# A chunked attention with a gated feed-forward: decay rows stored at a step of 6656 bytes, and a new order of the opening

## The chip, the cores and the metric

The kernel runs on one core of one Trainium2 chip. TensorE (PE in the views) multiplies, VectorE (DVE), ScalarE (ACT) and GpSimd (POOL) work on elements, SyncE (SP) issues transfers, and 16 DMA engines carry them from the device's memory. The metric is the device time of one execution in microseconds (us).

## The reference

An attention with decays runs over 4 batches, 8 heads and 768 tokens with 48 channels each. Its output, laid out as 3072 tokens of 384 channels, goes through a gated feed-forward of 1536 hidden channels, whose three weight matrices arrive as float64.

```python
for t in range(S):
    cur = np.einsum('bhd,bhe->bhde', u[None] * kt, vt)
    y[:, :, t] = np.einsum('bhd,bhde->bhe', rt, state + cur)
    state = wt[:, :, :, None] * state + np.einsum('bhd,bhe->bhde', kt, vt)
...
gate = 1.0 / (1.0 + np.exp(-(x @ w_gate)))
val = x @ w_val
return (gate * val @ w_out).astype(np.float32)
```

## The kernel before

The tokens are cut into 24 chunks of 128 (6 of each batch; chunk q belongs to batch q mod 4). A chunk needs two transfers: `pin` (decays, k and r, channel by channel, 112 rows of 1544 floats, 675.5 KB, L281) and `tok` (r, k and v token by token, 576 KB, L286). On VectorE it costs a scan, a reciprocal and a product (L321, L325, L327), a second scan and product (L338, L343), a reduction `a` for the bonus (L310), two masks `at` (L402), the state (L432), two `bon` (L448) and the rest of x (L466). On TensorE it costs `pk`, the sums `pv`, the scores `pa` (L370, L380), the value product and the transposed x.

The feed-forward goes by words: word f is 128 of the 1536 hidden channels with all three matrices, 1152 KB of float64. VectorE rebuilds float32 from the bits in `full` (L251, L255, L259). ScalarE checks the word's range (the guard, L245 and L246) and casts it to its high part (L264), VectorE subtracts that for the low part (`w`, L267), and then the word is ready. Every product is three matmuls of high and low parts: `pg` and `pu` (L474) against x, the sigmoid `sg` of `pg` on ScalarE (L485), its product with `pu` on VectorE (L492, named sg too), the high part `hh` on ScalarE (L496), the low part `hl` on VectorE (L500), and `po` on TensorE (L509).

Chunks 0 to 12 and the feed-forward of the first 8 chunks' rows form the opening, some 245 us. There the feed-forward works on two chunks at a time (`GROUPS`, four half groups), beside the words' arrival. After it a hand-written loop takes four chunks' rows at once with the next chunks' attention woven in.

The opening's order comes from a planner, class `Plan`. Each step is given to it with its engine, a cost in us, the steps that it needs, the buffers that it takes and gives back (`ROOM`) and a rank. The planner plays time forward: an engine that is free takes the step of lowest rank whose needs are met and whose buffers are free, and writes its instructions. So the costs and ranks set each engine's fixed order, and nothing else in the program. `TURNS` gives the ranks of chunks (c) and words (w), `LAGS` those of the four half groups, and `COMES` the order in which SP issues the transfers (p is pin, t is tok, w a word). SP issues them in just that order: one that waits for a buffer (two of pin, two of tok; a word has its own) holds up all behind it. On the chip each engine executes its list in order and waits by semaphore for the others.

In the lists of steps below a name carries the chunk's or the word's number and, behind a low line, a number of the program: full2_441 belongs to word 2, eg3_518 to chunk 3, a02_425 is `a` of chunk 2 (its tile is called a0), x0 holds the rows of chunks 0 to 3. sg0_0_3 and hl0_0_3 are the first half group (chunks 0 and 1) and word 3. Decays, k and r lie in the array `dec`, which the host writes ahead of the launch; the function `kernel` packs it.

Of the kernel before, what the change touches and what calls it, by code (L numbers as in the profile page):

```python
# [34 lines left out]
COMES = "p0 t0 ub w0 p1 p2 t1 w1 w2 p3 t2 t3 w3 w4 w5 t4 p4 w6 w7 w8 w9 w10 w11 p5 t5 t6 p6 t7 p7 p8 t8 t9 p9 p10 p11 t10 t11 p12 p13 t12 t13"
GROUPS = [(0, 0, 2), (0, 2, 4), (1, 0, 2), (1, 2, 4)]
LAGS = [0, 6.5, 15, 16]
ROOM = dict(pin=2, tok=2, bon=2, eg=1, ready=2, mid=2, kT=1, at=1, bank=2, x=2, full=1, pg=1, pu=1, unit=4, po0=1, po1=1, po2=1, po3=1)
HC = C // 2
HALVES = [slice(0, HC), slice(HC, C)]  # L40
# [4 lines left out]
def general(ctx: ExitStack, tc: tile.TileContext, dec, tok, wts, u, out, whi, wlo, ident):  # L45
# [44 lines left out]
    values = tok.rearrange("(b c) t (n p o e) -> c n o t b p e", b=B, n=3, o=2, e=D)  # L90
    for c in range(NC_):
        for b in range(B):
            nc.sync.dma_start(d[:, b], dec[b * NC_ + c])
        with tc.For_i(0, C) as i:
            def at(first, step):
                return d[:, :, first:first + NP * step].rearrange("a b (p c) -> a b p c", c=step)[:, :, :, bass.ds(i, 1)].broadcast_to(shape)
            for o in range(2):
                for b in range(B):
                    nc.sync.dma_start(vb[64 * o:64 * o + D, b], values[c, 2, o, bass.ds(i, 1), b].partition_broadcast(D))
            nc.vector.tensor_tensor(out=kv, in0=vb, in1=at(WW, C), op=ALU.mult)  # L100
            nc.vector.tensor_tensor(out=mix, in0=kv, in1=ub, op=ALU.mult)
# [90 lines left out]
def tile_kernel(ctx: ExitStack, tc: tile.TileContext, dec: bass.AP, tok: bass.AP, wts: bass.AP, u: bass.AP, out: bass.AP):  # L192
# [79 lines left out]
    def place(q):  # L272
        return q % B * NC_ + q // B

    def load_pin(q):
        t = p2.tile([L, WW + 2 * NP * C], F32, tag="pin", name=f"pin{q}")
        if q == 0:
            nc.sync.dma_start(t[:, :WW], dec[place(q)][:, :WW])
            nc.sync.dma_start(t[:, WW:], dec[place(q)][:, WW:])
        else:  # L280
            nc.sync.dma_start(t, dec[place(q)])  # L281
        pin[q] = t

    def load_tok(q):
# [253 lines left out]
    add("ub", "SP", 0.6, [], comes["ub"], lambda: nc.sync.dma_start(ub, u.partition_broadcast(P)))  # L538
    for q in range(3 * B + 2):
        k = rank.get(f"c{q}", 99)  # L540
        add(f"pin{q}", "SP", 2.4, [], comes[f"p{q}"], load_pin, q, take=["pin"])
        add(f"tok{q}", "SP", 2.1, [], comes[f"t{q}"], load_tok, q, take=["tok"])
        if q > 3 * B:
            continue
        add(f"b1_{q}", "POOL", 1.0, [f"tok{q}", "ub"], k, bonus1, q, take=["bon"])
        add(f"b2_{q}", "POOL", 1.0, [f"b1_{q}"], k, bonus2, q)
        add(f"b3_{q}", "DVE", 0.55, [f"b2_{q}"], k + 0.3, bonus3, q)
        add(f"b4_{q}", "POOL", 0.83, [f"b3_{q}"], k, bonus4, q)
        add(f"pk{q}", "DVE", 2.07, [f"pin{q}"], k, prep_k, q, take=["eg"])
        old = q >= B  # L550
        if old:
            add(f"fade{q}", "DVE", 0.36, [f"pk{q}", f"keep{q - B}"], k + 0.05, fade, q, take=["ready"])
        add(f"pr{q}", "DVE", 1.93, [f"pk{q}"], k + 0.1, prep_r, q)
        add(f"guard{q}", "ACT", 1.26, [f"pr{q}", old and f"fade{q}"], k + 0.5, guard, q, give=["eg"])
        if q == 3 * B:
            continue
        add(f"tk{q}", "PE", 0.4, [f"pk{q}"], k + 0.1, turn_k, q, take=["bank", "kT"])
        add(f"kT{q}", "ACT", 0.52, [f"tk{q}"], k + 0.1, take_k, q, give=["bank"])
        add(f"sm{q}", "PE", 0.55, [f"kT{q}", f"tok{q}"], k + 0.15, sums, q, take=["bank", "bank"], give=["kT"])
        add(f"mid{q}", "DVE" if old else "ACT", 0.36, [f"sm{q}", old and f"fade{q}"], k + 0.12, middle, q, take=["mid"], give=["bank"])  # L560
        add(f"keep{q}", "DVE", 0.36, [f"mid{q}"], k + 0.15, keep, q, give=["bank"])
        add(f"sc{q}", "PE", 1.1, [f"pr{q}", f"mid{q}"], k + 0.2, scores, q, take=["bank", "bank", "at"], give=["pin"] + ["ready"] * old)
        add(f"m0{q}", "DVE", 0.42, [f"sc{q}"], k + 0.2, mask, q, 0)
        add(f"m1{q}", "DVE", 0.42, [f"m0{q}"], k + 0.2, mask, q, 1)
        add(f"mx{q}", "PE", 0.5, [f"m1{q}"], k + 0.3, mix, q, give=["at"])
        add(f"mid{q}done", None, 0, [f"sc{q}", f"keep{q}"], k, give=["mid"])
        add(f"y0{q}", "DVE", 0.36, [f"mx{q}", f"b4_{q}"], k + 0.3, take_y, q, 0, give=["bank"])
        add(f"y1{q}", "DVE", 0.36, [f"y0{q}"], k + 0.3, take_y, q, 1, give=["bank"])
        first = q % B == 0
        add(f"tx{q}", "PE", 0.33, [f"y1{q}", q % B and f"tx{q - 1}"], k + 0.4, turn_x, q, take=["bank"] + ["x"] * first, give=["bon"])  # L570
        add(f"xh{q}", "ACT", 0.68, [f"tx{q}"], k, take_x, q)
        add(f"xl{q}", "DVE", 0.56, [f"xh{q}"], k, rest_x, q, give=["bank"])
        add(f"tok{q}done", None, 0, [f"mx{q}", f"sm{q}", f"b4_{q}", q % B and f"tok{q - 1}done"], k, give=["tok"])
    for f in range(NFF):
        k = rank[f"w{f}"]
        add(f"words{f}", "SP", 4.2, [], comes[f"w{f}"], fetch, f)
        add(f"wg{f}", "ACT", 2.8, [f"words{f}", f and f"wg{f - 1}"], k, w_guard, f)
        add(f"wb{f}", "DVE", 0.76, [f"words{f}", f and f"wb{f - 1}"], k, w_body, f, take=["full"])
        add(f"ws{f}", "DVE", 1.36, [f"wb{f}"], k, w_sign, f)
        add(f"wt{f}", "DVE", 1.36, [f"ws{f}"], k, w_tail, f)  # L580
        add(f"wh{f}", "ACT", 1.15, [f"wt{f}", f"wg{f}"], k, w_hi, f)
        add(f"wl{f}", "DVE", 1.3, [f"wh{f}"], k, w_lo, f, give=["full"])
# [101 lines left out]
```

## Time and profile before

| | |
|---|---|
| median of 3 runs | 605.04 us (603.53 to 608.01) |
| the profiled execution | 603.9 us, of which the span is 602.2 |
| TensorE busy | 558.7 us, 93% of the span |
| VectorE busy | 332.6 us, 55% |
| ScalarE busy | 201.6 us, 33% |
| GpSimd busy | 96.7 us, 16% |
| moved by DMA | 50.85 MB |

The profile is one execution, taken by the hardware profiler. Busy time is a sum over stages of different character, so a share of the whole span says little about one stage; the windows of the trace give the same by stretches. A wait in the timeline of an engine stands in brackets behind the instruction that waited, with what ended it. An instruction's duration can overlap the next one's start by some hundredths of a us.

### The profile page before, as it was taken

To read this page: it belongs to the slowest core of one execution; us is meant where nothing else is said; L and a number is where in the kernel's file an instruction comes from. 1 tells how busy PE (TensorE), PEld (TensorE's weight loads), DVE (VectorE), ACT (ScalarE), POOL (GpSimd) and SP (SyncE) were. 2 spreads that over 40 slices of the span, in tenths; PEclk is the share of its full clock that TensorE was granted. 3 is DMA by queue.
4 is the path that set the end of the run, shared out by engine and by line. 5 is a ranking of instruction groups with operands and counts; after the bars stand their busy time and mean duration, and the time that the engine had idled before them with its cause. 6 is when DMAs were issued, how large, how long until landed. Compare 5 with 4: busy or idle time off the path is not lost. (4 is left out here: it accounts for less than half of the span.)

```text
span 602.2 us, 14593 instructions
## 1 busy us (share of the span) xinstructions
PE 558.7 (93%) x6474; PEld 498.4 (83%) x6474; DVE 332.6 (55%) x570; ACT 201.6 (33%) x402; POOL 96.7 (16%) x86
## 2 busy tenths in 40 slices
PE   4475899999999999899999999999999999999994
PEld 3365799999999999788888888888888888888883
DVE  4989879989685653254554554554454453221220
ACT  3648683444333322312222322222321221222212
POOL 3352111102120502002201211211211210000000
PEclk9999699999999999999999999999999999999997
DMA  8788920033233130122033033022033000100001
GB/s 250 250 327 290 347 95 1 1 87 83 72 121 126 50 125 3 53 86 86 3 87 87 28 112 86 2 86 87 35 106 87 1 1 2 54 1 0 1 1 57
DMA packets 12055, 50.85 MB, mean 84 GB/s; under 512 B 1376, under 2 KB 4576, under 8 KB 10448
## 3 DMA queue, kind: packets, MB, share of 16 engines
q1 hardware_dynamic: 8528, 45.11, 23.4%
q10 hardware_dynamic: 3456, 4.72, 2.2%
q8 instruction: 53, 0.87, 0.6%
q14 instruction: 18, 0.15, 0.1%
HBM read 45.11 MB, written 4.72 MB: 83 GB/s over the span
## 5 line engine op out<-in xcount | busy, mean ns | idle before, releaser
L474 PE MATMUL pg<-x,w 128*128 128x256 f32 (+1 forms) x864 | 171.6, 344 | 2.1 <-DVE w L267 2.1
L474 PE MATMUL pu<-x,w 128*128 128x256 f32 (+1 forms) x864 | 170.5, 342 | 0.0
L474 PEld LDWEIGHTS pg<-x,w 128*128 128x128 f32 x864 | 138.3, 193 | 17.8 <-DVE w L267 2.2
L474 PEld LDWEIGHTS pu<-x,w 128*128 128x128 f32 x864 | 136.2, 191 | 17.3
L509 PE MATMUL po<-w,hh 128*128 128x384 f32 x576 | 147.7, 337 | 0.0
L492 DVE TENSOR_TENSOR sg<-pu,sg 128x256 f32<-128x256 f32 (+1 forms) x96 | 53.4, 557 | 149.9 <-PE pu L474 148.9
L509 PE MATMUL po<-w,hl 128*128 128x384 f32 x288 | 101.2, 351 | 7.1 <-DVE hl L500 7.0
L496 ACT CAST hh<-sg 128x256 fp32r<-128x256 f32 (+1 forms) x96 | 49.2, 512 | 170.0 <-DVE sg L492 169.6
L509 PEld LDWEIGHTS po<-w,hh 128*128 128x128 f32 x576 | 105.0, 189 | 0.9
L485 ACT ACTIVATE sg<-pg 128x256 f32<-128x256 f32 (+1 forms) x96 | 46.9, 488 | 141.7 <-PE pg L474 140.1
L314 POOL TENSOR_TENSOR bon<-tok,a 128x384 f32<-128x384 f32 x24 | 35.0, 1457 | 282.7 <-DVE a L310 282.7
L500 DVE TENSOR_TENSOR hl<-sg,hh 128x256 fp32r<-128x256 f32 (+1 forms) x96 | 55.7, 580 | 39.0 <-ACT hh L496 39.0
L509 PEld LDWEIGHTS po<-w,hl 128*128 128x128 f32 x288 | 54.3, 189 | 10.4 <-DVE hl L500 8.4
L303 POOL TENSOR_TENSOR bon<-tok,ub 128x384 f32<-128x384 f32 x24 | 32.6, 1358 | 113.4 <-DMA tok<-tok 61.1
L448 DVE TENSOR_TENSOR bon<-pa,bon 128x192 f32<-128x192 f32 x48 | 15.6, 353 | 49.3 <-PE pa L441 49.2
L348 ACT ACTIVATE junk<-eg 112x1032 bf16<-112x1032 f32 x24 | 25.6, 1066 | 30.7 <-DVE eg L338 30.6
L321 DVE TENSOR_TENSOR_SCAN eg<-pin,ends 112x516 f32<-112x516 f32 x24 | 30.0, 1251 | 4.9 <-DMA pin<-dec 4.9
L338 DVE TENSOR_TENSOR_SCAN eg<-pin,heads 112x516 f32<-112x516 f32 x24 | 30.5, 1270 | 0.0
L353 PE MATMUL pk<-ident,pin 112*128 112x112 f32 x96 | 14.7, 278 | 14.1 <-DVE pin L327 10.2
L306 POOL TENSOR_TENSOR bon<-bon,tok 128x384 f32<-128x384 f32 x24 | 27.3, 1136 | 1.7
L441 PE MATMUL pa<-tok,at 64*32 64x48 f32 x1536 | 23.8, 213 | 2.3 <-DVE at L402 2.3
L353 PEld LDWEIGHTS pk<-ident,pin 112*128 112x128 f32 x96 | 11.5, 150 | 17.1 <-issue 9.0
(62 smaller groups left out, 433.8 us busy)
## 6 DMA issues: line engine op xcount, KB each, us to landing
pin<-dec SPq DMA_DIRECT2D x23, 675.5 KB, 5.8
tok<-tok SPq DMA_DIRECT2D x24, 576.0 KB, 5.8
wraw<-wts SPq DMA_DIRECT2D x12, 1152.0 KB, 12.3
y<-o ACTq DMA_DIRECT2D x24, 192.0 KB, 1.9
pin<-dec SPq DMA_DIRECT2D x1, 448.0 KB, 4.3
pin<-dec SPq DMA_DIRECT2D x1, 227.5 KB, 2.9
ub<-u SPq DMA_DIRECT2D x1, 192.0 KB, 6.7
```

What stands on the lines that cost most here:

```text
L303: nc.gpsimd.tensor_tensor(out=bon[q], in0=tk[q][:, 0:DM], in1=ub, op=ALU.mult)
L306: nc.gpsimd.tensor_tensor(out=bon[q], in0=bon[q], in1=tk[q][:, DM:2 * DM], op=ALU.mult)
L314: nc.gpsimd.tensor_tensor(out=by_head(bon[q]), in0=by_head(tk[q][:, 2 * DM:]), in1=a0, op=ALU.mult)
L321: nc.vector.tensor_tensor_scan(out=e[:, 516:0:-1], data0=t[:, 516:0:-1], data1=ends[:, 516:0:-1], initial=0.0, op0=ALU.mult, op1=ALU.add,)
L338: nc.vector.tensor_tensor_scan(out=e[:, WW:WW + 516], data0=t[:, 0:516], data1=heads[:, 0:516], initial=0.0, op0=ALU.mult, op1=ALU.add,)
L353: nc.tensor.transpose(out=t[:, p * L:(p + 1) * L], in_=kk(q)[:, p], identity=ident[:L, :L])
L474: nc.tensor.matmul(t, lhsT=w[f][:, cols], rhs=x[n][:, a, k, i0 * C:i1 * C], start=k == 0 and j == 0, stop=k == NKT - 1 and j == 2)
L485: nc.scalar.activation(sg, hid["g", n, f, i0], AF.Sigmoid)
L492: nc.vector.tensor_tensor(out=sg, in0=hid["u", n, f, i0], in1=sg, op=ALU.mult)
L496: nc.scalar.copy(hh, hid["s", n, f, i0])
L500: nc.vector.tensor_tensor(out=hl, in0=hid["s", n, f, i0], in1=hid["hi", n, f, i0].bitcast(F32), op=ALU.subtract)
L509: nc.tensor.matmul(po[n, i][:, :DM], lhsT=h[:, c], rhs=w[f][:, 2 * DM:], start=f == 0 and j == 0, stop=f == NFF - 1 and j == 2,)
```

## The change

The rows of `dec` are padded from 1544 floats to `WR` = 1664, so that they begin 6656 bytes apart and not 6176 (13 x 512 bytes); the loads cut the pad off again. The order is made anew with other ranks (`TURNS`, `COMES`, `LAGS`) and other costs of three kinds of transfer in the planner (pin 2.4 to 2.6, tok 2.1 to 1.8, word 4.2 to 3.0). Each engine executes the same instructions as before, in another order. The line numbers of the changed kernel are one higher (L267 becomes L268).

```diff
@@ -27,14 +27,15 @@
 L = 112
 W1 = C + 1
 WW = 520
+WR = 1664
 NFF = DFF // P
 NKT = DM // P
 TINY = 2.0 ** -14
 LEAST = float.fromhex("0x1.2p-15")
-TURNS = "c0 w0 c1 w1 c2 w2 w3 w4 w5 c3 w6 w7 w8 c4 w9 w10 w11 c5 c6 c7 c8 c9 c10 c11 c12"
-COMES = "p0 t0 ub w0 p1 p2 t1 w1 w2 p3 t2 t3 w3 w4 w5 t4 p4 w6 w7 w8 w9 w10 w11 p5 t5 t6 p6 t7 p7 p8 t8 t9 p9 p10 p11 t10 t11 p12 p13 t12 t13"
+TURNS = "c0 w0 w1 c1 w2 c2 w3 w4 c3 w5 w6 w7 w8 c4 w9 w10 w11 c5 c6 c7 c8 c9 c10 c11 c12"
+COMES = "p0 ub t0 w0 p1 t1 p2 w1 w2 p3 t2 t3 w3 w4 w5 t4 w6 p4 w7 w8 w9 w10 t5 p5 t6 p6 p7 w11 t7 p8 t8 t9 p9 p10 t10 t11 p11 p12 t12 t13 p13"
 GROUPS = [(0, 0, 2), (0, 2, 4), (1, 0, 2), (1, 2, 4)]
-LAGS = [0, 6.5, 15, 16]
+LAGS = [0, 9.0, 15.5, 14.5]
 ROOM = dict(pin=2, tok=2, bon=2, eg=1, ready=2, mid=2, kT=1, at=1, bank=2, x=2, full=1, pg=1, pu=1, unit=4, po0=1, po1=1, po2=1, po3=1)
 HC = C // 2
 HALVES = [slice(0, HC), slice(HC, C)]
@@ -90,7 +91,7 @@
     values = tok.rearrange("(b c) t (n p o e) -> c n o t b p e", b=B, n=3, o=2, e=D)
     for c in range(NC_):
         for b in range(B):
-            nc.sync.dma_start(d[:, b], dec[b * NC_ + c])
+            nc.sync.dma_start(d[:, b], dec[b * NC_ + c][:, :WW + 2 * NP * C])
         with tc.For_i(0, C) as i:
             def at(first, step):
                 return d[:, :, first:first + NP * step].rearrange("a b (p c) -> a b p c", c=step)[:, :, :, bass.ds(i, 1)].broadcast_to(shape)
@@ -276,9 +277,9 @@
         t = p2.tile([L, WW + 2 * NP * C], F32, tag="pin", name=f"pin{q}")
         if q == 0:
             nc.sync.dma_start(t[:, :WW], dec[place(q)][:, :WW])
-            nc.sync.dma_start(t[:, WW:], dec[place(q)][:, WW:])
+            nc.sync.dma_start(t[:, WW:], dec[place(q)][:, WW:WW + 2 * NP * C])
         else:
-            nc.sync.dma_start(t, dec[place(q)])
+            nc.sync.dma_start(t, dec[place(q)][:, :WW + 2 * NP * C])
         pin[q] = t
 
     def load_tok(q):
@@ -538,8 +539,8 @@
     add("ub", "SP", 0.6, [], comes["ub"], lambda: nc.sync.dma_start(ub, u.partition_broadcast(P)))
     for q in range(3 * B + 2):
         k = rank.get(f"c{q}", 99)
-        add(f"pin{q}", "SP", 2.4, [], comes[f"p{q}"], load_pin, q, take=["pin"])
-        add(f"tok{q}", "SP", 2.1, [], comes[f"t{q}"], load_tok, q, take=["tok"])
+        add(f"pin{q}", "SP", 2.6, [], comes[f"p{q}"], load_pin, q, take=["pin"])
+        add(f"tok{q}", "SP", 1.8, [], comes[f"t{q}"], load_tok, q, take=["tok"])
         if q > 3 * B:
             continue
         add(f"b1_{q}", "POOL", 1.0, [f"tok{q}", "ub"], k, bonus1, q, take=["bon"])
@@ -573,7 +574,7 @@
         add(f"tok{q}done", None, 0, [f"mx{q}", f"sm{q}", f"b4_{q}", q % B and f"tok{q - 1}done"], k, give=["tok"])
     for f in range(NFF):
         k = rank[f"w{f}"]
-        add(f"words{f}", "SP", 4.2, [], comes[f"w{f}"], fetch, f)
+        add(f"words{f}", "SP", 3.0, [], comes[f"w{f}"], fetch, f)
         add(f"wg{f}", "ACT", 2.8, [f"words{f}", f and f"wg{f - 1}"], k, w_guard, f)
         add(f"wb{f}", "DVE", 0.76, [f"words{f}", f and f"wb{f - 1}"], k, w_body, f, take=["full"])
         add(f"ws{f}", "DVE", 1.36, [f"wb{f}"], k, w_sign, f)
@@ -664,10 +665,10 @@
         o[:, 64:64 + D] = a[:, 1]
         return o
 
-    dec = np.zeros((NG, L, WW + 2 * NP * C), np.float32)
+    dec = np.zeros((NG, L, WR), np.float32)
     dec[:, :, :NP * W1].reshape(NG, L, NP, W1)[..., 1:] = lanes(inputs["w"], 1.0)
     dec[:, :, WW:WW + NP * C] = lanes(inputs["k"], 0.0).reshape(NG, L, -1)
-    dec[:, :, WW + NP * C:] = lanes(inputs["r"], 0.0).reshape(NG, L, -1)
+    dec[:, :, WW + NP * C:WW + 2 * NP * C] = lanes(inputs["r"], 0.0).reshape(NG, L, -1)
     rows = [inputs[n].transpose(0, 2, 1, 3).reshape(NG, C, H * D) for n in ("r", "k", "v")]
     tok = np.ascontiguousarray(np.concatenate(rows, axis=2))
     ups = [inputs[n].reshape(NKT, P, NFF, P).transpose(2, 1, 0, 3).reshape(NFF, P, DM) for n in ("moe_w_gate", "moe_w_val")]
```

SP's order is the string `COMES`, word for word. Of VectorE's list three places follow, before and then now.

First, the start, from chunk 0's bonus `a` (the seventh step): `at0` are chunk 0's masks, `full0` is word 0.

```order
L310 TENSOR_REDUCE a00_177<-bon0_124 128x8
L402 TENSOR_TENSOR at0_150<-pa0_0_151,after_85 128x256
L402 TENSOR_TENSOR at0_150<-pa0_1_152,after_85 128x256
L251 TENSOR_SCALAR full0_187<-wraw0_113 128x1152
L448 TENSOR_TENSOR bon0_124<-pa0_0_151,bon0_124 128x4x48
L255 SCALAR_TENSOR_TENSOR full0_187<-wraw0_113,full0_187 128x1152
```

```order
L311 TENSOR_REDUCE a00_152<-bon0_122 128x8
L252 TENSOR_SCALAR full0_182<-wraw0_113 128x1152
L403 TENSOR_TENSOR at0_154<-pa0_0_155,after_85 128x256
L256 SCALAR_TENSOR_TENSOR full0_182<-wraw0_113,full0_182 128x1152
L403 TENSOR_TENSOR at0_154<-pa0_1_156,after_85 128x256
L260 SCALAR_TENSOR_TENSOR full0_182<-wraw0_113,full0_182 128x1152
```

Word 0's first two steps stand between and ahead of the masks now; they stood behind them.

Second, around the first hidden rows, from chunk 1's x (step 36 before, 39 now) to sg0_0_0.

```order
L466 TENSOR_TENSOR x0_233<-px1_377,x0_233 128x3x128
L267 TENSOR_TENSOR w1_373<-full1_312,w1_373 128x1152
L310 TENSOR_REDUCE a02_425<-bon2_382 128x8
L432 TENSOR_TENSOR state2_101<-pv2_1_393,mid2_421 112x192
L251 TENSOR_SCALAR full2_441<-wraw2_277 128x1152
L492 TENSOR_TENSOR sg0_0_0_427<-pu0_0_0_429,sg0_0_0_427 128x256
L255 SCALAR_TENSOR_TENSOR full2_441<-wraw2_277,full2_441 128x1152
L500 TENSOR_TENSOR hl0_0_0_487<-sg0_0_0_427,hh0_0_0_475 128x256
```

```order
L467 TENSOR_TENSOR x0_252<-px1_390,x0_252 128x3x128
L260 SCALAR_TENSOR_TENSOR full2_378<-wraw2_254,full2_378 128x1152
L433 TENSOR_TENSOR state2_101<-pv2_1_403,mid2_430 112x192
L311 TENSOR_REDUCE a02_435<-bon2_376 128x8
L322 SCALAR_TENSOR_TENSOR eg3_447<-pin3_322,ends_80 112x516
L326 RECIPROCAL heads_83<-eg3_447 112x4
L328 TENSOR_TENSOR pin3_322<-pin3_322,eg3_447 112x512
L493 TENSOR_TENSOR sg0_0_0_454<-pu0_0_0_437,sg0_0_0_454 128x256
```

Behind that x stand word 1's L260, the state, `a` and the three first steps of chunk 3 now; before it was word 1's last step, `a`, the state and the first step of word 2.

Third, around word 4's last step, w4, up to sg0_0_4; the step ahead of the first row of each list is word 4's L259 (L260).

```order
L448 TENSOR_TENSOR bon3_423<-pa3_0_669,bon3_423 128x4x48
L333 TENSOR_TENSOR ready4_768<-state0_99,eg4_664 112x192
L448 TENSOR_TENSOR bon3_423<-pa3_1_670,bon3_423 128x4x48
L338 SCALAR_TENSOR_TENSOR eg4_664<-pin4_612,heads_83 112x516
L343 TENSOR_TENSOR pin4_612<-pin4_612,eg4_664 112x512
L500 TENSOR_TENSOR hl0_0_3_789<-sg0_0_3_728,hh0_0_3_784 128x256
L267 TENSOR_TENSOR w4_786<-full4_712,w4_786 128x1152
L466 TENSOR_TENSOR x0_233<-px3_780,x0_233 128x3x128
L251 TENSOR_SCALAR full5_814<-wraw5_516 128x1152
L310 TENSOR_REDUCE a04_826<-bon4_619 128x8
L255 SCALAR_TENSOR_TENSOR full5_814<-wraw5_516,full5_814 128x1152
L492 TENSOR_TENSOR sg0_0_4_828<-pu0_0_4_816,sg0_0_4_828 128x256
```

```order
L403 TENSOR_TENSOR at3_689<-pa3_0_690,after_85 128x256
L501 TENSOR_TENSOR hl0_0_3_743<-sg0_0_3_718,hh0_0_3_738 128x256
L403 TENSOR_TENSOR at3_689<-pa3_1_691,after_85 128x256
L334 TENSOR_TENSOR ready4_754<-state0_99,eg4_685 112x192
L268 TENSOR_TENSOR w4_741<-full4_683,w4_741 128x1152
L449 TENSOR_TENSOR bon3_395<-pa3_0_690,bon3_395 128x4x48
L252 TENSOR_SCALAR full5_803<-wraw5_452 128x1152
L449 TENSOR_TENSOR bon3_395<-pa3_1_691,bon3_395 128x4x48
L256 SCALAR_TENSOR_TENSOR full5_803<-wraw5_452,full5_803 128x1152
L339 SCALAR_TENSOR_TENSOR eg4_685<-pin4_624,heads_83 112x516
L344 TENSOR_TENSOR pin4_624<-pin4_624,eg4_685 112x512
L493 TENSOR_TENSOR sg0_0_4_813<-pu0_0_4_822,sg0_0_4_813 128x256
```

Word 4's last step is step 78 and not 81; chunk 4's second scan and product stand behind it, and chunk 3's two `bon` too.

## Rows read from the trace of the kernel before

**Rows 1.** The page of the kernel before: its span, and of each engine the busy time, share of the span and instructions.

```profile
span 602.2 us, 14593 instructions
...
PE 558.7 (93%) x6474; PEld 498.4 (83%) x6474; DVE 332.6 (55%) x570; ACT 201.6 (33%) x402; POOL 96.7 (16%) x86
```

**Rows 2.** Windows of the same trace, 13 to 75 us and 75 to 150 us: length; of each engine the busy time and (instructions); granted TensorE clock, DMA share, GB/s.

```profile
13.00:75.00 62.00, 39.71 (x636) 35.16 (x629) 55.27 (x77) 41.51 (x73) 17.44 (x12) 0.92 0.86 302
...
75.00:150.00 75.00, 74.29 (x973) 71.59 (x972) 67.55 (x107) 36.52 (x75) 10.47 (x9) 1.00 0.18 54
```

**Rows 3.** What VectorE (DVE) waited for between 13 and 75 us: the waiting tile and line, the one waited for, and us in total, times, longest.

```profile
DVE sg L492 <- PE pu L474: 4.2, 3, 1.8
DVE bon L448 <- PE pa L441: 0.9, 2, 0.5
DVE at L402 <- PE pa L380: 0.9, 1, 0.9
DVE x L466 <- ACT x L462: 0.4, 1, 0.4
DVE full L251 <- DMA wraw<-wts: 0.4, 1, 0.4
```

**Rows 4.** Transfers, view of stretches. First line: 57.9 to 66.9 us, in which words alone are moved (queue, packets, MB, share of the 16 engines' time). Second: 204.5 to 210 us, in which one pin alone is moved. Third: 13 to 18 us, a mix of pins, tokens and words. The last two: what was issued between 46.2 and 48.3 us (bytes of each, us from issue to landing): word 6 and pin 4.

```profile
q1 hardware_dynamic: 462, 3.77, 100.3%
...
q1 hardware_dynamic: 128, 0.69, 44.2%
...
q1 hardware_dynamic: 240, 1.17, 98.9%
...
wraw<-wts SPq DMA_DIRECT2D x1, 1152.0 KB, 9.9
pin<-dec SPq DMA_DIRECT2D x1, 675.5 KB, 8.1
```

**Rows 5.** Timeline of VectorE: start in us, duration in us, engine, line, operation, out<-in, shape, and in brackets the idle time before it with what ended it.

```profile
11.87 0.76 DVE L402 TENSOR_TENSOR at<-pa,after 128x256 f32<-128x256 f32 x2 [0.22 <-PE pa L380]
13.01 0.76 DVE L251 TENSOR_SCALAR full<-wraw 128x1152 int32<-128x1152 int32 x1 [0.39 <-DMA wraw<-wts]
...
37.94 0.54 DVE L310 TENSOR_REDUCE a<-bon 128x8 f32<-128x384 f32 x1
38.41 0.34 DVE L432 TENSOR_TENSOR state<-pv,mid 112x192 f32<-112x192 f32 x1
...
40.93 0.43 DVE L492 TENSOR_TENSOR sg<-pu,sg 128x256 f32<-128x256 f32 x1 [1.42 <-PE pu L474]
41.27 1.35 DVE L255 SCALAR_TENSOR_TENSOR full<-wraw,full 128x1152 int32<-128x1152 int32 x1
...
42.87 0.42 DVE L402 TENSOR_TENSOR at<-pa,after 128x256 f32<-128x256 f32 x1
...
46.39 0.18 DVE L325 RECIPROCAL heads<-eg 112x4 f32<-112x4 f32 x1
46.49 0.66 DVE L327 TENSOR_TENSOR pin<-pin,eg 112x512 f32<-112x512 f32 x1
...
57.43 1.22 DVE L321 TENSOR_TENSOR_SCAN eg<-pin,ends 112x516 f32<-112x516 f32 x1
...
65.07 0.42 DVE L492 TENSOR_TENSOR sg<-pu,sg 128x256 f32<-128x256 f32 x1 [1.77 <-PE pu L474]
...
67.21 0.35 DVE L448 TENSOR_TENSOR bon<-pa,bon 128x192 f32<-128x192 f32 x1
...
68.74 0.69 DVE L343 TENSOR_TENSOR pin<-pin,eg 112x512 f32<-112x512 f32 x1
...
69.68 1.35 DVE L267 TENSOR_TENSOR w<-full,w 128x1152 fp32r<-128x1152 f32 x1
70.95 0.55 DVE L466 TENSOR_TENSOR x<-px,x 128x384 fp32r<-128x384 f32 x1
...
74.91 0.42 DVE L492 TENSOR_TENSOR sg<-pu,sg 128x256 f32<-128x256 f32 x1 [1.01 <-PE pu L474]
...
130.27 0.75 DVE L251 TENSOR_SCALAR full<-wraw 128x1152 int32<-128x1152 int32 x1
```

**Rows 6.** Timeline of ScalarE (ACT), 62.5 to 68.5 us, the same columns: the guard of word 7 (L245 is its first half; the second, L246, ends where hh begins), the hi part of hidden rows of word 3, the cast of word 4.

```profile
63.36 1.27 ACT L245 ACTIVATE sq<-wraw 128x1152 f32<-128x1152 f32 x1
...
65.92 0.39 ACT L496 CAST hh<-sg 128x256 fp32r<-128x256 f32 x1
66.80 1.16 ACT L264 CAST w<-full 128x1152 fp32r<-128x1152 f32 x1 [0.49 <-DVE full L259]
```

**Rows 7.** Timeline of SyncE's queue (SP): start and duration of issues.

```profile
46.67 1.39 SPq L281 DMA_DIRECT2D pin<-dec  x1
48.10 3.79 SPq L238 DMA_DIRECT2D wraw<-wts  x6
```

**Rows 8.** Windows of 3 us around the fall of the clock; columns as in rows 2.

```profile
58.00:61.00 3.00, 0.94 (x34) 0.81 (x24) 2.97 (x6) 2.92 (x5) 0.00 (x0) 0.85 1.03 430
61.00:64.00 3.00, 3.00 (x15) 3.00 (x16) 2.31 (x4) 0.92 (x2) 0.00 (x0) 0.50 1.01 414
64.00:67.00 3.00, 2.40 (x69) 1.99 (x68) 1.93 (x4) 2.48 (x6) 0.00 (x0) 0.51 1.02 427
```

**Rows 9.** Timeline of TensorE: the score matmuls of chunk 5.

```profile
115.36 0.70 PE L370 MATMUL pa<-pin 48*64 48x64 f32 x32
```

## The prediction

> **What bounds the kernel now.** I read the page first: of a span of 602.2 us TensorE is busy for 558.7, so 43.5 us of its time are idle [rows 1]. The windows then say where [rows 2]. Between 13 and 75 us VectorE is busy for 55.27 of 62 us and TensorE for 39.71; between 75 and 150 us TensorE is busy for 74.29 of 75. So two stages with two limits: up to 75 us VectorE, which rebuilds the weights and serves the chunks, sets the pace; after that TensorE has work in store and a VectorE that comes a little sooner or later is worth nothing. The change moves steps of the first stage and leaves the second's amount of work alone, so only what it does ahead of 75 us counts.
>
> What VectorE waits for in that stage stands in the view of its waits [rows 3]: 4.2 us for the product `pu` in TensorE (3 times), 0.9 and 0.9 us for a chunk's score and value matmuls, 0.4 us for ScalarE's copy of x, and 0.4 us for a transfer. They sum to 6.8 us. The last is the only transfer that it waits for there; transfers do not pace VectorE as it stands.
>
> **The padded rows.** The same 6176 bytes of each row are read, by the same instructions; only the address of the next row moves. The trace of before has no row at the new step, so I bound its price. Words alone go at 2.39 us per MB (100.3% of 9.0 us for 3.77 MB) and a lone chunk of decays at 44.2% of 5.5 us for 0.69 MB, 2.43 us, or 3.5 us per MB; in a mixed stretch it is 4.2 us per MB (98.9% of 5.0 us for 1.17 MB) [rows 4]. If the new step brought the chunks to the words' rate, each would take 0.69 x 2.39 = 1.65 us, 0.8 us less alone and 0.69 x (4.2 - 2.39) = 1.25 us less in the mix. That is the upper end; the lower is a loss, which I set at the same 0.8 us for each, since nothing in the rows excludes that rows further apart are read more slowly. I take 0: the nearest row is the lone chunk's, and nothing in it tells the step of the rows from the 112 of them or their length as the reason for the rate. The cover is VectorE's own work, since it waited 0.4 us for transfers; without that cover the five chunks of the opening would be worth 5 x 0.8 = 4.0 to 5 x 1.25 = 6.3 us.
>
> The Trainium skill, page "DMA: Bandwidth & Descriptors", section "How a descriptor splits into AXI transactions", says that reads go in transactions that start on 256-byte borders, and that a row which starts off such a border fetches the unused bytes below its start as well. By it a row of 6176 bytes is 193 beats of 32 bytes, the old step adds up to 7 of them and 3.5 on average, and the new step none if the array begins on a border: an estimate of 1.8%, or 0.04 us of 2.43. That speaks against a large gain from the padding; no run so far shows it, and the sum would be the same to 0.2 us.
>
> **The order of VectorE.** Both lists hold the same steps, and by the step `hl0_0_4` (number 88 in both, a little after 75 us) the same work has been done. So a word that is put 1 or 2 us further up is no gain of that size by itself: something else is put back by as much. What can change is VectorE's idle time ahead of that step. I go through the waits, with the durations of [rows 5]: `full` (L251) at 0.76 us, L255 and L259 (the same operation on the same shape) at 1.35, each of a chunk's two scans at 1.22. Of the change, lines count one more (L256 is L255).
>
> *sg0_0_0* waited 1.42 us at 40.93. It needs word 0 and the x of chunk 1. Between that x and it stood w (1.35), a (0.54), state (0.34), full (0.76) = 2.99 us; now L260 of the word (1.35), state (0.34), a (0.54) and chunk 3's scan, reciprocal and product (1.22 + 0.18 + 0.66) = 4.29 us. The 1.30 us more hide all but 0.12 of the wait.
> *sg0_0_3* waited 1.77 us at 65.07, and its TensorE chain starts with word 3. Between word 3 and it stood at, full, at, L255 = 0.42 + 0.76 + 0.42 + 1.35 = 2.95 us; now state, full, scan, reciprocal, product, L256 = 0.34 + 0.76 + 1.22 + 0.18 + 0.66 + 1.35 = 4.51: 1.56 us of the wait go.
> *sg0_0_4* waited 1.01 us at 74.91. Between word 4 and it stood x, full, a, L255 = 0.55 + 0.76 + 0.54 + 1.35 = 3.20 us, now bon, full, bon, L256, scan, product = 0.35 + 0.76 + 0.35 + 1.35 + 1.22 + 0.69 = 4.72: the whole 1.01 goes.
> The chunks' waits: between chunk 1's second product and its first mask stand 4.89 us (x, full, a, L256, state, L260) where 1.64 stood (state, a, full), ahead of the steps `bon` of chunks 0 and 1 a word's L260 (1.35) for its `full` (0.76), and 3.26 for 1.35, and ahead of chunk 0's x 3.26 for 1.35; each is longer by more than the wait, so 0.9 + 0.9 + 0.4 = 2.2 us go too. Together 1.30 + 1.56 + 1.01 + 2.2 = **6.1 us** that could go.
>
> What comes in their place:
> 1. *At the start* word 0's `full` now stands ahead of chunk 0's two masks. The word landed at 13.01, and the masks filled 11.87 to 12.6 [rows 5]; they now come after it, so **0.76 us** are lost. Chunk 0's tokens now go behind the u row, 0.2 MB, about 0.5 us at the words' rate; the step that they hold up (state) was followed by a wait for GpSimd, which needs u anyway, so that costs 0. Tokens of chunk 1 are now sent ahead of the wait for a buffer; should they share the queues with word 0, it lands up to 0.59 x 2.39 = 1.4 us later. I keep that for the range.
> 2. *ScalarE.* The hi part of word 3's first hidden rows (`hh0_0_3`) stands on ScalarE behind the guard of word 7, and word 4's cast behind that; this is so in both lists. Word 6 landed 9.9 us after its issue at 48.1 [rows 4, 7], so at 58.0, and a word takes 2.82 us (1.18 MB at 2.39): word 7 at 60.8, whichever way round pin 4 and word 6 go. The guard takes from 63.36 to 65.92, 2.6 us, the hi cast 0.3 to the next start, word 4's cast 1.16 [rows 6]. So word 4 cannot be closed ahead of 60.8 + 2.6 + 0.3 + 1.16 = 64.9, where its last step stood at 69.68 [rows 5]. Of these 4.8 us 2.1 come from its new place alone (scan 1.22, product 0.69 and two bon of 0.35 go behind it, one a of 0.54 ahead). That leaves 2.7 us of VectorE's waits that can be cashed up to there, and 1.0 behind it (sg0_0_4): 3.7 in place of 6.1 - 0.76 = 5.3, so this wait gives back **1.6 us**.
> 3. *New hand-overs.* A VectorE that is some 3 us ahead meets TensorE's and ScalarE's short chains of other steps sooner: word 3 and word 4 now have about 2 us between their L260 and their last step, and x of chunk 2 1.8 us behind its bon. These are bounded by 0 and by the whole 3.7 us; I take the nearest thing that the trace shows, the chunks' waits of the same stage, **2.2 us**.
> 4. *Queues.* Pin 4 now waits on SP behind word 6: it landed 8.1 us after its issue at 46.7 [rows 4, 7], at 54.8; 2.8 us later is 57.6. VectorE took it at 57.43 and will at about 57.43 + 2.65 (word 3's last step, word 4's `full` and one `a` go ahead of the scan: 1.35 + 0.76 + 0.54) less what it has gained by then, 1.3 + 2.2 - 0.76 = 2.7; so it may wait 0.3 us, inside item 3's bounds. Pin 5 lands some 3 us sooner than it did. The added lags and planner's costs put out no instruction of their own.
>
> **The sum.** 603.9 us (profiled; span 602.2 and 1.7 around it) - 6.1 + 0.76 + 1.6 + 2.2 = **602.4 us**. Beside it the runs of before have a median of 605.04 (603.53 to 608.01), 1.1 above the profiled one.
>
> **The rivals.**
> A. *All waits close.* If the padded rows do go faster, words 6 and 7 land sooner, ScalarE's wait of item 2 goes, and VectorE runs through: 603.9 - 5.3 = 598.6 us. For it: the rate of 3.5 against 2.39 us per MB. Against it: VectorE would have to meet no new wait at all in 60 us. Chance 0.15.
> B. *Nothing net.* The waits only change places: 603.9 + 0.76 = 604.7 us at most 606 with the late word 0. For it: VectorE is busy for 55.27 of 62 us and its work is the same. Chance 0.24.
> C. *The clock.* TensorE was granted half speed from 61 to 67 us (0.50 and 0.51, the 1.2 GHz level), after a stretch of 3 us in which it was busy for 0.94, and was busy for 5.40 us at that level [rows 8]. If earlier words keep it busy and it stays at 2.4 GHz, half of that, 2.7 us, is saved on top of the forecast: 599.7 us. Against it: before word 3 it still has little to do. Chance 0.04.
> D. *Slower.* Word 11 now stands on SP behind pin 7, which waits for a buffer that chunk 5's score matmuls give free; in the trace they ran from 115.36 [rows 9]. Pin 7 issued at about 116.6 and landing as late as 8.1 us, with the word 2.8 behind it, gives 127.5; VectorE took word 11 at 130.27 [rows 5]. So the slack is about 3 us; if chunk 5's scores come more than 3 us later, every further microsecond stalls VectorE, behind which stand the hidden rows that TensorE needs, and from 10 us on the kernel is over 611. Against it: its decays land sooner now. Chance 0.07.
>
> **The numbers.** The forecast has 0.50, with 600.2 to 604.6 as its own range (item 3 at 0 and at twice 2.2). A change of about 1% (599.0 and 611.1 around the median) is what a measurement of this kernel can tell from none. Faster by more: A and a part of C, 0.17. Slower by more: D, 0.07. Within: 0.76. The range takes in A, B and C and the spread of the runs about them, 597.5 to 607.5.
>
> **What would show it.** VectorE's waits between 13 and 75 us fall from 6.8 to about 4 us, those for `pu` from 4.2 to under 1; a wait for ScalarE's hh or w is new; VectorE's first word starts at 13.0 with the masks behind it; word 4's last step starts near 66; DMA's price for a lone chunk stays at 2.4 us. I am wrong if that price falls to 1.7 us (A), if the waits are as long as before in other places (B), or if word 11 is waited for (D).

## The result and the profile after

The changed kernel takes 609.32 us (median of 20 runs, 605.22 to 614.19) against 605.28 of before (20 runs): a ratio of 1.0067, 95% interval 1.0045 to 1.0089. It is 4 us slower. Forecast were 602.4 us and a range up to 607.5. The profiled execution took 608.9 us, 5.0 more than the one of before.

The page and the windows of the changed kernel (columns as in [rows 1] and [rows 2]):

```profile
span 607.1 us, 14586 instructions
...
PE 561.2 (92%) x6474; PEld 500.3 (82%) x6474; DVE 334.1 (55%) x570; ACT 201.4 (33%) x402; POOL 98.3 (16%) x86
...
13.00:75.00 62.00, 39.25 (x632) 33.74 (x631) 52.67 (x75) 39.60 (x68) 17.75 (x13) 0.89 0.79 267
75.00:150.00 75.00, 73.04 (x904) 70.64 (x903) 69.47 (x107) 36.53 (x76) 13.34 (x9) 1.00 0.22 69
```

TensorE stands idle 45.9 us in place of 43.5, and between 75 and 150 us it now idles for 2.0 us where it idled for 0.7. VectorE, meant to wait less between 13 and 75 us, is busy for 52.67 us, not 55.27. Its waits there, to be held against [rows 3]:

```profile
DVE bon L449 <- PE pa L442: 2.3, 2, 1.9
DVE eg L322 <- DMA pin<-dec: 2.3, 1, 2.3
DVE full L252 <- DMA wraw<-wts: 1.8, 1, 1.8
DVE a L311 <- POOL bon L307: 1.2, 1, 1.2
DVE sg L493 <- PE pu L475: 0.8, 2, 0.6
DVE at L403 <- PE pa L381: 0.7, 1, 0.7
DVE hl L501 <- ACT hh L497: 0.6, 2, 0.4
DVE state L433 <- ACT mid L427: 0.2, 1, 0.2
```

The waits for `pu` fell from 4.2 us to 0.8, as worked out. But the sum went from 6.8 us to 9.9: 2.3 for pin 4 (eg, L322), 1.8 for word 0, 1.2 for GpSimd's bonus and 2.3 for the value matmuls (`bon`) stand in their place. Where pin 4 was lost is read on SP. First the kernel before (start, duration, what is issued; the two issues behind these are [rows 7]), then the changed one:

```profile
27.24 0.33 SPq L281 DMA_DIRECT2D pin<-dec  x1
27.68 3.53 SPq L286 DMA_DIRECT2D tok<-tok  x2
31.26 1.38 SPq L238 DMA_DIRECT2D wraw<-wts  x3
46.24 0.33 SPq L286 DMA_DIRECT2D tok<-tok  x1
```

```profile
30.72 0.33 SPq L282 DMA_DIRECT2D pin<-dec  x1
31.15 4.20 SPq L287 DMA_DIRECT2D tok<-tok  x2
35.40 1.55 SPq L239 DMA_DIRECT2D wraw<-wts  x3
50.96 0.33 SPq L287 DMA_DIRECT2D tok<-tok  x1
51.33 1.16 SPq L239 DMA_DIRECT2D wraw<-wts  x1
52.59 0.37 SPq L282 DMA_DIRECT2D pin<-dec  x1
```

Pin 3 (the first row of each) goes out 3.5 us later. It waits for the buffer that chunk 1's score matmuls give back; chunk 1's first mask, which waits for the same matmuls, starts at 30.68 us where it started at 27.21. The tokens behind it wait for chunk 1's value matmuls, and these for the second mask, which starts at 32.96 us and not at 28.81; so words 3 to 5 go out 4.1 us later. Tokens 4 wait for chunk 2's value matmuls, 4.7 us later. Ahead of that issue the DMA engines have next to nothing to do (DMA share is the last column but one):

```profile
46.00:49.00 3.00, 3.00 (x26) 3.00 (x25) 2.17 (x5) 2.97 (x7) 0.00 (x0) 1.00 0.08 34
49.00:52.00 3.00, 3.00 (x79) 2.60 (x78) 2.96 (x5) 2.97 (x7) 0.00 (x0) 1.00 0.12 20
```

GpSimd begins chunk 4's bonus, for which VectorE then waits 1.2 us, when tokens 4 have landed:

```profile
56.01 1.02 POOL L304 TENSOR_TENSOR bon<-tok,ub 128x384 f32<-128x384 f32 x1 [10.41 <-DMA tok<-tok]
```

Then pin 4 goes out behind word 6, at 52.59 and not 46.67 [rows 7], and lands 11.1 us later at 63.7; before it was 54.8. VectorE stands before it:

```profile
60.30 1.12 DVE L252 TENSOR_SCALAR full<-wraw 128x1152 int32<-128x1152 int32 x1
63.72 1.23 DVE L322 TENSOR_TENSOR_SCAN eg<-pin,ends 112x516 f32<-112x516 f32 x1 [2.31 <-DMA pin<-dec]
...
66.93 0.42 DVE L493 TENSOR_TENSOR sg<-pu,sg 128x256 f32<-128x256 f32 x1
...
69.30 0.42 DVE L501 TENSOR_TENSOR hl<-sg,hh 128x256 fp32r<-128x256 f32 x1 [0.35 <-ACT hh L497]
```

Behind the scan of chunk 4 stands sg0_0_3, which TensorE has had ready since 65.4 us (64.08 + 1.33, below); it begins at 66.93, and TensorE waits 4.37 us for the `hl` made from it. Before, TensorE waited 1.59 us at this place (first row; the other two are of the changed kernel):

```profile
69.82 0.44 PE L509 MATMUL po<-w,hl 128*128 128x384 f32 x1 [1.59 <-DVE hl L500]
...
64.08 1.33 PE L475 MATMUL pu<-x,w 128*128 128x256 f32 x9
69.78 0.69 PE L510 MATMUL po<-w,hl 128*128 128x384 f32 x1 [4.37 <-DVE hl L501]
```

The clock comes on top. Windows around the stretches in which TensorE was granted about half speed, 1.2 GHz, before and then changed:

```profile
60.00:66.40 6.40, 5.64 (x82) 5.23 (x82) 4.63 (x7) 4.14 (x8) 0.00 (x0) 0.51 1.00 416
70.30:73.70 3.40, 3.40 (x16) 3.40 (x15) 3.40 (x5) 1.10 (x3) 0.92 (x1) 0.50 1.00 227
```

```profile
57.00:64.00 7.00, 5.55 (x92) 4.73 (x90) 3.55 (x5) 4.04 (x7) 3.72 (x4) 0.52 1.00 272
67.00:74.00 7.00, 4.22 (x72) 3.67 (x73) 4.69 (x10) 5.83 (x10) 0.00 (x0) 0.51 0.91 378
251.40:254.60 3.20, 3.01 (x9) 2.82 (x10) 0.13 (x1) 0.96 (x2) 0.00 (x0) 0.52 0.09 32
```

Before, TensorE was busy for 9.04 us at that level; half of it, 4.5 us, is an estimate of what that costs. Now it is 12.78 us, 6.4. The third stretch is new. It lies at the end of the opening, 250 us in, where TensorE had stood idle for 2.08 us ahead of it:

```profile
247.23 0.34 PE L510 MATMUL po<-w,hl 128*128 128x384 f32 x1
...
248.28 1.23 PE L475 MATMUL pu<-x,w 128*128 128x256 f32 x9
251.59 0.69 PE L510 MATMUL po<-w,hl 128*128 128x384 f32 x1 [2.08 <-DVE hl L501]
```

The sigmoid that goes with the `pu` at 248.28 had to wait behind the two output copies on ScalarE, which wait for the product at 247.23:

```profile
248.90 0.48 ACT L516 COPY o<-po 128x384 f32<-128x384 f32 x1 [0.47 <-PE po L510]
...
249.80 0.38 ACT L486 ACTIVATE sg<-pg 128x256 f32<-128x256 f32 x1 [0.42 <-ACT o L516]
```

Before, TensorE idled twice at this place, 1.21 and 1.48 us with a busy 2.4 us between, and its clock stayed at full speed:

```profile
243.92 0.44 PE L509 MATMUL po<-w,hl 128*128 128x384 f32 x1 [1.21 <-DVE hl L500]
...
247.77 0.44 PE L509 MATMUL po<-w,hl 128*128 128x384 f32 x1 [1.48 <-DVE hl L500]
```

Windows over the whole opening close the account, before and changed:

```profile
0.00:75.00 75.00, 44.78 (x726) 39.34 (x727) 60.87 (x86) 44.70 (x78) 22.79 (x29) 0.93 0.85 293
75.00:240.00 165.00, 163.59 (x2330) 156.58 (x2329) 122.53 (x222) 65.47 (x148) 30.83 (x26) 1.00 0.23 70
240.00:260.00 20.00, 17.31 (x240) 14.73 (x239) 4.90 (x12) 5.25 (x12) 0.00 (x0) 1.00 0.17 53
```

```profile
0.00:75.00 75.00, 43.25 (x708) 37.18 (x709) 57.52 (x82) 42.79 (x73) 22.91 (x29) 0.91 0.80 263
75.00:240.00 165.00, 161.69 (x2311) 154.64 (x2310) 126.26 (x224) 66.03 (x149) 32.36 (x26) 1.00 0.27 84
240.00:260.00 20.00, 17.92 (x165) 16.43 (x163) 3.57 (x8) 5.52 (x13) 0.00 (x0) 0.91 0.11 40
```

TensorE's idle time goes from 30.2 to 31.75 us up to 75 us, from 1.4 to 3.3 up to 240, and from 2.7 to 2.1 at the end of the opening: 2.8 us more. With 1.9 us of clock that makes 4.7 of the 4.9 us between the spans. The windows lie at fixed times and so hold not quite the same work; over the whole spans TensorE is busy for 2.5 us more and idle for 2.4 us more.

### The profile page after: what moved, and what is told of

Its sections match the earlier page's. It is cut to its first block, busy times and chain, and to the rows that moved or that the text cites. A ratio compares the mean times of both kernels' runs of the same rounds, so it can differ in the third digit from the quotient of the medians.

```text
span 607.1 us, 14586 instructions
## 1 busy us (share of the span) xinstructions
PE 561.2 (92%) x6474; PEld 500.3 (82%) x6474; DVE 334.1 (55%) x570; ACT 201.4 (33%) x402; POOL 98.3 (16%) x86
## 5 line engine op out<-in xcount | busy, mean ns | idle before, releaser
L322 DVE TENSOR_TENSOR_SCAN eg<-pin,ends 112x516 f32<-112x516 f32 x24 | 29.9, 1246 | 6.5 <-DMA pin<-dec 6.5
L307 POOL TENSOR_TENSOR bon<-bon,tok 128x384 f32<-128x384 f32 x24 | 28.6, 1193 | 1.9
L442 PEld LDWEIGHTS pa<-tok,at 64*32 64x32 f32 x1536 | 20.0, 114 | 8.9 <-DVE at L403 6.1
```

The source lines that it names most:

```text
L307: nc.gpsimd.tensor_tensor(out=bon[q], in0=bon[q], in1=tk[q][:, DM:2 * DM], op=ALU.mult)
L322: nc.vector.tensor_tensor_scan(out=e[:, 516:0:-1], data0=t[:, 516:0:-1], data1=ends[:, 516:0:-1], initial=0.0, op0=ALU.mult, op1=ALU.add,)
L442: nc.tensor.matmul(bank["y", q, o][some, p], lhsT=att[q][half, o, p, i:i + 32], rhs=values(q, p, o, half), start=q < B and not s and p == ...
```

## The experiments

In most kernels below the planner only plans, and a new function writes its lists out, so that SP's order, the number of buffers or the place of one step can be changed with all other lists kept. Line numbers are then about 24 higher. The diffs below show pieces of the edits.

| run | lists of the engines | SP's order | also | ratio to before, 95% |
|---|---|---|---|---|
| e1 | before | before | padded | 1.0001 (0.9983 to 1.0018) |
| e2 | new | new | not padded | 1.0063 (1.0036 to 1.0090) |
| e3 | new | before | | 1.0069 (1.0047 to 1.0091) |
| e4 | before | new | | 1.0041 (1.0024 to 1.0059) |
| e5 | new | new, pin 4 ahead of word 6 | | 1.0050 (1.0025 to 1.0076) |
| e6 | new | new | 3 token buffers | 1.0015 (0.9990 to 1.0040) |
| e7 | new | new, old start | | 1.0080 (1.0053 to 1.0106) |
| e8 | before | before | 3 token buffers | 1.0000 (0.9977 to 1.0023) |
| e9 | new | new | end, product moved | 1.0093 (1.0057 to 1.0128) |
| e10 | before | before | end closed up | 0.9971 (0.9952 to 0.9990) |
| e11 | new | new | chunk 1, two steps up | 1.0094 (1.0065 to 1.0124) |
| e12 | new | new | e6, e9 and e11 | 1.0013 (0.9983 to 1.0043) |
| e13 | new | new | chunk 1, three steps up | 1.0102 (1.0064 to 1.0140) |
| e14 | new | new | end, copies moved too | 1.0063 (1.0039 to 1.0087) |
| e15 | new | new | e13 and e14 | 1.0043 (1.0019 to 1.0066) |
| e16 | new | new | e15 and 3 token buffers | 0.9991 (0.9963 to 1.0019) |

**The two halves of the change.** e1 keeps the old tables and takes only the padding of the diff; e2 takes only the tables.

> The old order (TURNS, COMES, LAGS and costs of before) with only the rows of dec at a step of 6656 bytes. If the padded rows are read no faster and no slower, as the sum took it: ratio to before 1.000 within 0.002, a lone pin's packets at 2.4 us. If the padding is what made the change slower: ratio about 1.007, VectorE waiting longer for pins with the lists unchanged. If it speeds pins up to the words' rate: lone pin 1.65 us, ratio 0.995 or less.

> The new order of every engine with the rows of dec at the old step of 6176 bytes. If the order is the whole loss: ratio 1.005 to 1.009, as the change. If the padding is: 1.000. Theory in favour: the order, since in the changed kernel pin 4 came 8.9 us later and VectorE waited 2.3 us for it.

The padding is worth nothing that can be seen (within 0.2%), and the order alone shows the whole loss. In the changed kernel a lone pin takes 42.8% of 5.5 us, 2.35 us, against 2.43 [rows 4]:

```profile
q1 hardware_dynamic: 128, 0.69, 42.8%
```

**Lists and transfers apart.** e3 and e4 cross them:

```diff
-    plan.run()
+    order = plan.run()
+    plan.write(order, sends, ROOM)
```

> Padded; PE, VectorE, ScalarE and GpSimd keep the changed kernel's lists, SP sends in the order of before up to pin 7 (tokens 0 ahead of u, tokens 1 behind pin 2, pin 4 ahead of word 6, word 11 ahead of pin 5). Theory transfers (the new order of SP is the loss): ratio 1.000 or below, word 0 at 13.0, no wait for pin 4. Theory lists (chunk 1 put behind word 1 frees the pin buffer 3.5 us later, and all transfers behind pin 3 with it): ratio 1.003 to 1.007, pin 3 still issued at about 29 to 31 us and pin 4 still waited for.

> Padded; PE, VectorE, ScalarE and GpSimd keep the lists of before, SP sends in the changed order up to pin 7 (but word 11 behind word 10, where the old lists need it). Theory transfers: ratio 1.003 to 1.007. Theory lists: within 0.003 of before (a start about 1 us later through tokens 0 and word 0), pin 3 issued at about 27 to 28 us.

Each half alone is slower, and the two don't add up: SP's old order saves the new lists nothing. In e3 pin 3 went out at 29.06 and tokens 4 at 50.05 us, the stops were still there. e5 and e7 put back one piece of SP's order each; the piece of e5:

```diff
-t4 w6 p4 w7
+t4 p4 w6 w7
```

> The changed kernel with one swap in SP's order: pin 4 ahead of word 6, as before. Theory late pin 4 (VectorE stands 2.3 us at its scan, sg0_0_3 behind it is late, TensorE idles 4.4 us): pin 4 lands about 59.5 instead of 63.7, the wait goes, ratio 1.001 to 1.004. Rival lists (the place of the steps, not the transfer, sets the end): the wait goes and the time stays, 1.005 to 1.009.

> The changed kernel with the start of SP's order of before: tokens 0 ahead of u, tokens 1 behind pin 2. Word 0 lands at about 12.5 to 13 and not at 14.0, state of chunk 0 at 9.5 and not 11.1. Theory start: the 1 to 1.5 us go through to the end, ratio 1.004 to 1.005. Rival: VectorE has them back by word 1 (25.7 in both), ratio 1.006 to 1.007.

In e5 the wait for pin 4 is gone from VectorE's waits, but other waits stand in its place: between 13 and 81 us they sum to 11.1 us, against 9.9 in the changed kernel. The ratio is 0.0017 lower, less than the intervals can tell from none, so no gain from pin 4's place alone is shown. The old start gives back nothing, as the rival had it.

**SP's stops.** e6 leaves every list and SP's order as changed, and gives tokens a third buffer; e8 does so to the kernel before.

```diff
-tk[q] = p2.tile([P, 3 * DM], F32, tag="tok", name=f"tok{q}")
+tk[q] = toks.tile([P, 3 * DM], F32, tag="tok", name=f"tok{q}")
```

> The changed kernel's lists and SP order, with three token buffers instead of two, so that SP does not stop at tokens 3 and 4 for chunks 1 and 2. Theory SP stops (chunks 1 and 2 were put behind words 1 and 2, so buffers come free 3.5 to 4.7 us later and every transfer behind): pin 4 is issued at about 46 instead of 52.6 and lands at about 53, no wait for it, ratio 1.002 or less. Rival lists: transfers are early and the time stays, 1.004 to 1.008.

> The kernel before with three token buffers, lists and SP order unchanged. If its transfers were paced by nothing that matters (VectorE waited 0.4 us for transfers): 1.000 within 0.002. If SP's stop at tokens 3 and 4 costs it too: 0.995 to 0.998.

Pin 4 went out at 47.5 us, and VectorE's waits for pins are gone:

```profile
47.52 0.33 SPq L307 DMA_DIRECT2D pin<-dec  x1
```

VectorE's waits between 13 and 81 us sum to 8.1 us. The ratio falls by 0.0052, over 3 us of the 4 (the two intervals together leave 0.002 to 0.0085); before, the same buffer gave nothing. So the stops for token buffers are, by this estimate, the larger part of the loss, and only the new order has a loss there. Through which of the transfers behind the stop it comes is not shown: the profiled execution of e6 is its slowest, 609.19 us. A third buffer for pins was not tried.

**Which chunk stops SP.** e11 and e13 move steps of chunk 0 and 1 back up in the changed lists (e11 the first two):

```diff
+    ahead("xl0", "pr1")
+    ahead("mid1", "wg1")
+    ahead("keep1", "wb1")
```

> The changed kernel with two steps of chunk 0 and 1 moved back up: the x of chunk 0 ahead of chunk 1's second scan on VectorE (it holds one of two PSUM banks that chunk 1's sums need), and chunk 1's copy mid ahead of word 1's guard on ScalarE. Theory (chunk 1's lateness stops SP): chunk 1's scores about 2 us sooner, pin 3 issued at about 28.5 instead of 30.7, pin 4 about 2 us sooner, ratio 1.002 to 1.005. Rival: nothing of it arrives at pin 4, since chunk 2 stands behind word 2 too; ratio 1.006 to 1.007.

> The changed kernel with three steps moved up: x of chunk 0 ahead of chunk 1's second scan, copy mid of chunk 1 ahead of word 1's guard, and state of chunk 1 ahead of word 1's first step (in the run before this one the scores of chunk 1 waited 2.78 us for that state, so the first two moves gave nothing). Theory (chunk 1 put behind word 1 is what stops SP): masks of chunk 1 done at about 30 instead of 33, pin 3 issued at about 28.5 instead of 30.7, ratio 1.002 to 1.005. Rival (chunk 2 and tokens 4 set the stop in any case): pin 3 early, pin 4 still after 61 us and waited for, ratio 1.006 to 1.009.

The rival holds. SP in e13: pin 3 goes out at 28.12 as meant, but tokens 3, words 3 to 5 and tokens 4 go out as late as in the changed kernel, and pin 4 is waited for as before:

```profile
28.12 0.33 SPq L306 DMA_DIRECT2D pin<-dec  x1
28.55 6.37 SPq L311 DMA_DIRECT2D tok<-tok  x2
34.97 1.43 SPq L263 DMA_DIRECT2D wraw<-wts  x3
51.69 0.33 SPq L311 DMA_DIRECT2D tok<-tok  x1
...
53.23 0.37 SPq L306 DMA_DIRECT2D pin<-dec  x1
```

```profile
DVE eg L346 <- DMA pin<-dec: 2.7, 1, 2.7
```

So it is the value matmuls of chunks 1 and 2, which free the token buffers, that hold SP back, and not the scores that free pins. Both kernels are slower than the changed one, if anything.

**The end of the opening.** e10 moves one product in the kernel before; e9 does the like in the changed one, and e14 takes the output copies along (behind the sign # stand the runs that have the line).

```diff
+    ahead("dn3_10", "dn3_11")  # e10
+    ahead("dn3_11", "dn2_11")  # e9 and e14
+    ahead("out3_11", "dn2_11")  # e14
```

> The kernel before with its own end of the opening closed up: the fourth half group's down product of word 10 moved from ahead of its last pu to behind it. TensorE idles 1.21 and 1.48 us there at 243 and 247, never at half speed. Theory seam: one of the two waits goes, 1.2 to 1.5 us, ratio 0.9975. Rival: the longer single wait that is left makes the clock fall as in the changed kernel, ratio 1.000 to 1.001.

> The changed kernel with one step moved at the end of the opening: the last down product of the fourth half group (word 11) goes from ahead of the last pu of the third half group to behind it. In the changed kernel TensorE idles 2.08 us at 249.5 and is then granted half speed from 251.4 to 255, which costs 1.6 us more. Theory seam: the idle time falls below 1 us, no half speed there, ratio 1.003 to 1.005. Rival (the fall of the clock there has another cause): half speed stays, ratio 1.006 to 1.007.

> The changed kernel with the last down product of the fourth half group and its two output copies on ScalarE behind the last hidden rows of the third (the earlier move left the copies ahead of the last hh, so the wait of 2.3 us stayed). Theory seam: TensorE idles under 1 us at 248 to 251, no half speed at 251 to 255, 1.5 to 2.5 us gone, ratio 1.003 to 1.005. Rival: half speed stays, 1.006 to 1.009.

In e10 TensorE is idle for 0.17 of the 24 us between 240 and 264 us, where it was idle for 2.69 before, and the kernel is faster than both, 602.6 us against 604.39 of before in the same job. In e9 the last product still waited, 2.26 us, because `hh` now stood behind the copies, and half speed followed: nothing gained. e14 clears that; 0.4 us of waiting is left, and TensorE is at full speed (columns as in [rows 2]):

```profile
249.00:252.00 3.00, 2.56 (x14) 2.15 (x13) 0.42 (x1) 1.46 (x4) 0.00 (x0) 1.00 0.36 131
```

Its ratio still is 1.0063: the intervals of it and the changed kernel leave room for a gain of 0.003 or none, so from e14 alone nothing is settled. In the two other pairs that differ in the end alone, the ratio fell by 0.0029 (before to e10) and 0.0059 (e13 to e15).

**All together.**

> The changed kernel's order with three token buffers and both moves (seam, chunk 1). If the three causes are separate and are the whole loss: 1.0015 of three buffers, less 0.002 for the seam and up to 0.002 for chunk 1, so 0.997 to 1.000. If they are one and the same loss, or others remain: 1.001 to 1.003.

> Both moves of the two runs ahead in one kernel, two token buffers. If both causes hold and add up: 0.999 to 1.003. If only the seam holds: 1.003 to 1.006.

> As the run ahead, with three token buffers. If stops of SP and the seam are the whole loss, what is left is the forecast's gain: 0.996 to 0.999. If something else remains: 1.000 or more.

e12 has e9's move, which gained nothing. Its ratio leaves out four of twelve executions: one of 1877 us, and what that was is not known, and three of 611.9 to 613.2 us. With those three it would be about 1.004, so nothing is concluded from e12. e15 against e16 shows the third token buffer once more: 0.0052. With the stops and the end mended (and e13's three steps moved), e16 is at 0.9991. The old lists with the end closed are at 0.9971. So with both taken away the new lists show no gain over the old ones: the intervals overlap.

## Why the prediction was wrong

*The padding at 0*: right. The rate of a lone pin stayed, and e1 is at 1.0001. Rival A, which needed faster rows, had no ground.

*The estimate by the Trainium skill* (page "DMA: Bandwidth & Descriptors", section "How a descriptor splits into AXI transactions"): 0.04 us of 2.43 for each pin. The two rows differ by 0.08 us, which one transfer of each cannot tell from nothing; it agrees in that it is small.

*The waits for pu would close*: right for the waits (4.2 to 0.8 us, and none of 1.01 behind), wrong for what that is worth. They closed because VectorE came later to the hidden rows, with more put ahead of them: sg0_0_0 began at 44.83 us and not at 40.93, hl0_0_4 at 80.0 and not at 76.5. The hand-over then is waited for by TensorE (4.37 us at 69.78, 1.59 before). At hl0_0_4, where the forecast would have VectorE 1.5 us ahead by its sum, it is 3.5 us behind. The prediction counted VectorE's idle time as the whole price and did not look at what TensorE does meanwhile; here most of the closed waits were VectorE's for the engine that ends the kernel.

*The chunks' waits* (2.2 us) would close: about half did. Those for ScalarE's copy of x and ahead of chunk 1's `bon` are gone; chunk 1's first mask still waits 0.65 us (0.91 before) and chunk 0's `bon` 0.42 (0.53). A new one of 1.93 us stands ahead of chunk 3's `bon` at 73.64, whose masks the new list brings at 68.53 and 69.64 and not at 60.62 and 61.62.

*The start*: 0.76 us were charged, with 1.4 more as a bound. Word 0 landed 1.0 us later, the wait for it rose by 1.4 us. By e7, undoing it gives nothing back.

*ScalarE's guard*: 1.6 us were charged; the waits for `hh` came to 0.6. The chain was named rightly, but VectorE never came early enough for it.

***The queues: this is the step that failed.*** Item 4 let pin 4 slip by one word, 2.8 us, and charged 0.3 us. It took over the issue times of before. They hang on chunks 1 and 2, which the new list puts back, and with two token buffers SP stood still until 50.96 us. Tokens 4 went out 4.7 us later, and GpSimd's bonus, for which VectorE waits 1.2 us, began when they had landed. Pin 4 lost the same 4.7 us and 4.2 behind word 6, landed 8.9 us later, and was waited for 2.3 us. With a third token buffer and all lists kept, e6 gives back over 3 of the 4 us, and e16 against e15 as much again. The wait for pin 4 alone is not shown to be the price: e3 and e5 have none, and their ratios are 1.0069 and 1.0050. Which of the transfers behind the stop carries the loss stays open. The trace of before had the rows that would have told of the stops: SP's issues right behind the chunks' matmuls.

*"Only what it does ahead of 75 us counts"*: wrong too. The end of the opening is in the planner's tables as well. There a copy that a step issues on ScalarE, which the planner counts apart from it, held up the next sigmoid, and the clock fell. What that is worth is not settled: TensorE is idle for 0.6 us less there than before, half speed costs 1.5 us in the profiled execution, and e14, which closes the end, shows no clear gain.

*The rivals*: B was nearest (waits that change places), at 604.7 to 606. D forecast a slower kernel by word 11 late behind pin 7; word 11 was issued at 119.98, VectorE took it at 132.6 without a wait. The kernel became slower by a like means, transfers on SP behind one that waits for a buffer, at another place. The loss of 0.67% stays within the 1% that the forecast called the same.

Open besides are two things: why the old lists with the new SP order (e4) lose 0.4%, for which no run takes the start and pin 4 apart; and how much of the new lists' loss the clock makes by itself, since a profile shows one execution and the changed kernel's runs differ by 9 us. The mean granted clock, which is on record for each execution, gives an estimate: 0.984 over the 20 of the changed kernel and 0.987 over 115 of the kernel before that ran beside the experiments; 0.0028 of 607 us is 1.7 us, less than half of the 4.

## What to carry to other kernels

When a list of steps is reordered, follow each queue's stops first: which step frees the buffer that the queue's next transfer waits for, and where that step now stands. A wait that goes on an engine off the end's path is worth nothing if it went because that engine came later. One more buffer for the transfer that stops a queue, with all lists kept, tells whether the stops cost anything, if the gain is larger than the spread of the runs.

## What was not expected of the hardware

TensorE's clock after idle spells: at the end of the opening two spells of 1.21 and 1.48 us, or shorter ones, left the granted clock at full speed in all eight profiles that had them. One spell of 2.1 to 2.3 us was followed by half speed in eight of ten profiles (not in e2 and e13), 1.5 us lost in the changed kernel. In the changed kernel a gap that was shorter in sum (2.08 against 2.69 us) was followed by the fall. The length of one spell does not tell by itself: an idle spell of 3.14 us at 18 to 21 us in the changed kernel was followed by full speed (granted clock 1.00 from 0 to 57 us). Nor does this fall explain how the times spread: e14, whose profile has no such fall, has runs at 605.1 to 607.0 and at 609.6 to 610.8 with nothing between, and the mean granted clocks of the two groups (0.984 to 0.986, 0.980 to 0.988) overlap. What splits them is open.

Putting word 6 ahead of pin 4 cost pin 4 4.2 us (1.2 in the issue behind tokens 4, 3.0 from issue to landing), while a word takes 2.82 us among words. Why it is more is not shown.
